# A one-core decode kernel: the first loads split in another way, and the last weight in other chunks

## The chip, the cores and the metric

The kernel runs on one core of a Trainium2 chip. The metric is the device time of one execution in microseconds. A core has an engine for matrix products (PE; its weight loads are told apart as PEld), a vector engine (DVE), a scalar engine (ACT), GpSimd (POOL) and a sync engine (SP), which in this kernel issues nearly all transfers. Sixteen DMA engines per core carry the transfers. Each transfer from the SP queue is cut into rows, one contiguous row per partition, and the rows are dealt out over the sixteen engines. When an engine has written its share of a transfer it raises that transfer's semaphore; the transfer has landed when all sixteen have.

## What is computed

One token, `x` of 576 numbers, is normalised and goes through two branches whose results are added to it.

```
xn = layernorm(x)                                   # 576
q  = xn @ wq                                        # 576 x 4096: 32 heads of 128
k, v = last 4096 rows of the caches, 16 kv heads    # two q heads share a kv head
A  = softmax(q k^T / sqrt(128)) v  -> 4096  @ wo    # 4096 x 576
z  = gelu(xn @ w_in)                                # 576 x 4608, halves z1, z2 of 2304
B  = (z1 * (w_sp * layernorm(z2) + b_sp)) @ w_out   # 2304 x 576
out = x + A + B                                     # 576
```

All inputs are bf16. What has to be read from memory is 51 MB: `wq` 4.7 MB, `w_in` 5.3 MB, the windows of K and V 16.8 MB each, `wo` 4.7 MB and `w_out` 2.7 MB.

## The kernel before

**Tiles.** `wq_t` and `win_t` hold the two first weights with 128 partitions, one contiguous row of 36,864 or 41,472 bytes for each partition. K and V come in four pieces each, called quads (`kn0` to `kn3`, `v0` to `v3`), of four kv heads and 4 MB. A quad has 128 partitions with a row of 32,768 bytes each. The quads share a pool of three buffers, `kvpool`: K0, K1 and V0 take the three, and each later one waits until the buffer that it takes over has been read for the last time. `w_out` is held as two halves of nine rows per partition; the first half is one tile, the second is three tiles, by `WOUT_CHUNKS` (L38). `wo` is two tiles.

**Order of the transfers.** All of these are issued on SP's queue in the order in which the program names them. `load_rows` (L110 to L114) issues a weight in `parts` transfers, the f-th of which holds the partitions f, f + parts, and so on. `load_quad` (L94 to L99) does the same for a quad. The calls of L116 to L120 are the first nine transfers: `wq` in four, `w_in` in one, K0 in two, K1 in one, V0 in one. Three small loads (`xrow`, two elements of `sb_row`, L76 to L78) are issued on ACT's queue at the same time. Later, K2 is issued behind the first quad's work, V1 and K3 behind the second's, V2 and V3 behind the third's, and then the output weights in the order `w_out` first half, `wo` in two, `w_out` second half in three (L440 to L444).

**Semaphores.** The transfers of both queues take eight landing semaphores in turn. A transfer that takes one up again first waits, on the issuing engine, for the landing of the transfer that had it before. What stands behind it on that queue waits with it.

**Order of the work on PE.** PE and SP run in the order in which the program is written (`manual_schedule`, L107). PE makes the statistics of `x`, then `xn_times(wq_t, ...)` (L238), the columns of q (L244), `xn_times(win_t, ...)` (L257), the columns of z (L268), and then quad by quad the transposes of K (`transpose_k`, L328), the scores (L345), the transposes of the probabilities (L362) and the products with V (`pv`, L384). Filler products (`spin`, L455) stand at a few places behind the third quad. The end is `project` (L470), which adds one row of `wo` or `w_out` at a time, as two products, into two PSUM rows: `wo` in two chunks, then the second half of `w_out` chunk by chunk (L499, L500). Two casts (L503, L504) and one transfer of 1,152 bytes (L505) write the result.

Every product of `xn_times` contracts over all 128 partitions, so it needs every part of its weight, however this is split by partitions.

Of the kernel before, what the change touches and what calls it, by code (L numbers as in the profile page):

```python
# [34 lines left out]
NZ1 = 18  # L35
KV_BUFS = 3
WO_CHUNKS = ((0, 20), (20, 32))
WOUT_CHUNKS = ((0, 0, 9), (1, 0, 5), (1, 5, 8), (1, 8, 9))  # L38


@with_exitstack
def kernel(
# [14 lines left out]
    nc = tc.nc  # L57
    P = nc.NUM_PARTITIONS
# [26 lines left out]
    wq_t = wpool.tile([P, 9, 2048], BF16, name="wq")  # L85
    win_t = wpool.tile([P, 9, FH], BF16, name="win")
# [7 lines left out]
    def load_quad(cache, jq, nm, parts):  # L94
        tile_ = kvpool.tile([P, 128, DH], BF16, name=f"{nm}{jq}", tag="kv")
        dst, src = tile_[:].rearrange("p t d -> p (t d)"), quad_rows(cache, jq)
        for f in range(parts):
            nc.sync.dma_start(dst[f:P:parts, :], src[:, f:4:parts, :])
        return tile_  # L99

    def load_k(jq, parts=1):
        kn_tiles[jq] = load_quad(A_k_cache, jq, "kn", parts)

    def load_v(jq, parts=1):
        v_tiles[jq] = load_quad(A_v_cache, jq, "v", parts)
# [1 line left out]
    order = tc.manual_schedule(engines={PE, SP})  # L107
    ctx.enter_context(order)

    def load_rows(tile_, src, parts):  # L110
        for f in range(parts):
            nc.sync.dma_start(
                tile_[f:P:parts].rearrange("p k c -> p (k c)"),
                src.rearrange("m c -> (m c)").rearrange("(p n) -> p n", p=P)[f:P:parts, :])  # L114

    load_rows(wq_t, A_wq, 4)  # L116
    load_rows(win_t, B_w_in, 1)
    load_k(0, 2)
    load_k(1)
    load_v(0)  # L120


    ident = const.tile([P, P], BF16, name="ident")
# [185 lines left out]
    wout_sb = []  # L309
    for i, t0, t1 in WOUT_CHUNKS:  # L310
        n = (t1 - t0) * D
# [122 lines left out]
    def load_wout(n):  # L434
        i, t0, t1 = WOUT_CHUNKS[n]
        nc.sync.dma_start(  # L436
            wout_sb[n],
            B_w_out[ZC * i:ZC * (i + 1), :].rearrange("(p t) n -> p t n", t=9)[:, t0:t1, :])

    load_wout(0)  # L440
    for n, (r0, r1) in enumerate(WO_CHUNKS):
        nc.sync.dma_start(wo_sb[n][:], A_wo.rearrange("(p r) n -> p r n", r=32)[:, r0:r1, :])  # L442
    for n in range(1, len(WOUT_CHUNKS)):
        load_wout(n)  # L444
# [8 lines left out]
    def spin(n):  # L453
        for _ in range(n):
            nc.tensor.matmul(  # L455
                spare[:], lhsT=ident[:], rhs=q_bf[:].rearrange("p g c x -> p (g c x)"), start=True, stop=True)
# [17 lines left out]
    def project_b(n, ts):  # L474
        i, t0, t1 = WOUT_CHUNKS[n]
        for t in ts:
            k = 9 * i + t
            project(hv[:, k:k + 1], wout_sb[n][:, t - t0, :], last=(k == NZ1 - 1))
# [16 lines left out]
    for n, (r0, r1) in enumerate(WO_CHUNKS):  # L495
        for r in range(r0, r1):
            project(oT_all[:, r:r + 1], wo_sb[n][:, r - r0, :])
        spin((4, 0)[n])
    for n in range(1, len(WOUT_CHUNKS)):  # L499
        project_b(n, range(WOUT_CHUNKS[n][1], WOUT_CHUNKS[n][2]))  # L500

# [35 lines left out]
```

The softmax here doesn't subtract the row's maximum and nothing guards it: scores larger than these inputs give would overflow.

## Time and profile before

| what | value |
|---|---|
| time before, median of nine runs (lowest, highest) | 127.57 us (127.44, 127.79) |
| the profiled execution: its own time, its span | 127.79 us, 126.0 us |
| busy share of the span: PE, PEld, DVE, ACT, POOL | 74%, 53%, 35%, 32%, 2% |
| bytes moved, mean rate over the span | 51.11 MB, 406 GB/s |
| SP's queue: share of sixteen engines' span | 94.7% |
| mean granted clock of PE | 0.932 of full speed |

The span runs from the first instruction on the core to the last. Times inside it are counted from its start. The profile has a page with the shares, the span in forty slices, the DMA queues, the chain of work that ended last and the costliest groups of instructions. The trace behind it also gives what each engine and SP's queue waited for, a timeline, tables by stretch of time, and the start, length and size of every row that a DMA engine moved.

### The profile page before, as it was taken

What the parts mean: (1) busy time and instruction counts of PE and PEld (TensorE: products, weight loads), DVE (VectorE), ACT (ScalarE), POOL (GpSimd) and SP (SyncE); (2) the same over time, 40 slices, a digit from 0 to 9 for tenths busy, and PEclk for the clock granted to TensorE, in tenths of its full rate; (3) what the DMA queues carried; (4) which work ended last, traced back from release to release, by engine and by line L of the source; (5) the groups of instructions that cost most, each with busy time, mean ns of one, the idle gap of its engine ahead of it and who ended that gap; (6) DMA issues with size and microseconds to landing.
All of it is one profiled execution on the core that took longest, in us unless ns stands there. A gap on an engine that the chain in (4) does not pass through costs nothing.

```text
span 126.0 us, 2538 instructions
## 1 busy us (share of the span) xinstructions
PE 93.2 (74%) x1110; PEld 66.8 (53%) x1110; DVE 44.6 (35%) x127; ACT 40.9 (32%) x49; POOL 2.8 (2%) x10
## 2 busy tenths in 40 slices
PE   0110398358859999997967999506999999999982
PEld 0010138324859977885637785206878554554551
DVE  6062001102135364497539453452245245010001
ACT  3000001001003578876833679200656910100001
POOL 5010000000000000001000000000000000000000
PEclk9999999999855599999999999995599999999999
DMA  6889999979999899998999999999999999999960
GB/s 188 375 375 492 492 421 421 421 343 484 416 416 489 354 489 403 416 489 359 479 395 432 447 416 453 406 437 447 411 450 416 432 411 408 458 433 390 410 253 0
DMA packets 2386, 51.11 MB, mean 406 GB/s; under 512 B 326, under 2 KB 456, under 8 KB 712
## 3 DMA queue, kind: packets, MB, share of 16 engines
q1 hardware_dynamic: 2370, 50.96, 94.7%
q8 instruction: 8, 0.13, 0.4%
q14 instruction: 2, 0.02, 0.0%
q10 hardware_dynamic: 6, 0.00, 0.0%
HBM read 50.96 MB, written 0.00 MB: 404 GB/s over the span
## 4 chain that ended last, share of the span: by engine, by line
DMA 75%; PE 19%; ACT 2%; SPq 2%; issue 1%; ACTq 0%
DMA kn<-in_A_k_cache_dram 39%; DMA wout<-in_B_w_out_dram 32%; PE ktps L328 14%; DMA wq<-in_A_wq_dram 4%; PE sps L345 2%; ACT kT L332 1%; PE ops L384 1%; SPq L436 1%; PE fin L397 1%; SPq L442 1%; PE sps L470 1%; PE ptps L362 0%; ACT res L504 0%; ACTq L332 0%
## 5 line engine op out<-in xcount | busy, mean ns | idle before, releaser
L328 PE MATMUL ktps<-ident,kn 128*128 128x128 bf16 x512 | 35.9, 235 | 10.0 <-DMA kn<-in_A_k_cache_dram 9.2
L328 PEld LDWEIGHTS <-kn 128*128 128x128 bf16 x512 | 33.1, 106 | 14.8 <-DMA kn<-in_A_k_cache_dram 8.0
L332 ACT COPY kT<-ktps 128x1024 bf16<-128x1024 bf16 x32 | 31.3, 1014 | 24.1 <-PE ktps L328 24.1
L334 DVE COPY kT<-ktps 128x1024 bf16<-128x1024 bf16 x32 | 21.9, 689 | 20.5 <-PE ktps L328 20.5
L232 PEld LDWEIGHTS <-xz 128*32 128x32 bf16 x90 | 4.1, 140 | 13.9 <-issue 12.3
L345 PE MATMUL sps<-kT,q_bf 128*32 128x512 bf16 x128 | 10.7, 383 | 0.8 <-ACT kT L332 0.8
L232 PE MATMUL sps<-wq,xz 128*32 128x512 bf16 x36 | 4.5, 631 | 6.6 <-DMA wq<-in_A_wq_dram 6.6
L455 PE MATMUL spare<-q_bf,ident 128*128 128x512 bf16 x36 | 8.5, 380 | 0.0
L365 DVE TENSOR_TENSOR ptq<-ptps,own 128x128 bf16<-128x128 bf16 x32 | 4.6, 214 | 10.8 <-PE ptps L362 10.8
L384 PE MATMUL ops<-v,ptq 128*32 128x512 bf16 x128 | 8.2, 380 | 0.0
L371 DVE TENSOR_REDUCE psum_all<-ptq 128x8 f32<-128x1024 bf16 x4 | 7.9, 1971 | 0.1
L232 PE MATMUL zps<-win,xz 128*32 128x384 bf16 x54 | 4.3, 490 | 3.7 <-DMA win<-in_B_w_in_dram 3.7
L241 ACT COPY zrow<-sps 128x512 f32<-128x512 f32 x1 | 0.6, 585 | 15.9 <-PE sps L232 15.9
L455 PEld LDWEIGHTS <-ident 128*128 128x128 bf16 x36 | 3.2, 98 | 4.5 <-issue 1.2
L345 PEld LDWEIGHTS <-q_bf 128*32 128x32 bf16 x128 | 3.1, 94 | 4.4 <-issue 2.6
L390 ACT COPY on<-ops 128x512 f32<-128x512 f32 x4 | 2.3, 585 | 9.4 <-PE ops L384 9.4
L397 PE MATMUL fin<-on,sel 128*32 128x128 f32 x32 | 5.1, 312 | 0.3 <-ACT on L390 0.2
L384 PEld LDWEIGHTS <-ptq 128*32 128x32 bf16 x128 | 3.6, 96 | 3.1 <-issue 0.4
L504 ACT CAST res<-sps 1x320 bf16<-1x320 f32 x1 | 0.4, 416 | 14.6 <-PE sps L470 14.6
L268 PE MATMUL fin<-join,zrow 128*128 128x4 f32 x18 | 4.4, 379 | 0.9 <-DVE zrow L261 0.9
L268 PEld LDWEIGHTS fin<-join,zrow 128*128 128x128 f32 x18 | 4.4, 335 | 1.2 <-ACT zrow L260 1.2
L470 PE MATMUL sps<-wo,oT_all 128*1 128x256 bf16 (+1 forms) x64 | 4.7, 285 | 0.4 <-DMA wo<-in_A_wo_dram 0.2
(88 smaller groups left out, 50.1 us busy)
## 6 DMA issues: line engine op xcount, KB each, us to landing
v<-in_A_v_cache_dram SPq DMA_DIRECT2D x4, 4096.0 KB, 15.3
kn<-in_A_k_cache_dram SPq DMA_DIRECT2D x3, 4096.0 KB, 19.5
win<-in_B_w_in_dram SPq DMA_DIRECT2D x1, 5184.0 KB
wq<-in_A_wq_dram SPq DMA_DIRECT2D x4, 1152.0 KB, 8.7
kn<-in_A_k_cache_dram SPq DMA_DIRECT2D x2, 2048.0 KB, 31.6
wo<-in_A_wo_dram SPq DMA_DIRECT2D x1, 2880.0 KB
wo<-in_A_wo_dram SPq DMA_DIRECT2D x1, 1728.0 KB
wout<-in_B_w_out_dram SPq DMA_DIRECT2D x1, 1296.0 KB, 28.6
```

The source lines that it names most:

```text
L232: nc.tensor.matmul(banks[b][32 * i:32 * i + 32, 0:n], lhsT=xz[:, k, :], rhs=w[:, k, c0:c0 + n], start=(t == 0), stop=(k >= 7), tile_positi ...
L268: nc.tensor.matmul(fin[:, MZ + 4 * t:MZ + 4 * t + 4], lhsT=zv[:, t, :], rhs=join[:], start=True, stop=True,)
L328: nc.tensor.transpose(tps[:, s, :], kn[:, 32 * c + 8 * f + s, :], ident[:])
L332: nc.scalar.copy(kT[:], src)
L334: nc.vector.tensor_copy(kT[:], src)
L345: nc.tensor.matmul(sps[b][32 * i:32 * i + 32, :], lhsT=q_bf[:, g, c, :], rhs=parts[f // 2][:, 512 * (f % 2):512 * (f % 2) + 512], start=(c ...
L365: nc.vector.tensor_tensor(ptq[:, c, b, :, :].rearrange("p i (s x) -> p i s x", x=8), ptps[:, 4 * b:4 * b + 4, :].rearrange("p s (i r) -> p ...
L371: nc.vector.tensor_reduce(out=psum_all[:, 8 * g:8 * g + 8], in_=ptq[:].rearrange("p c b i (s x) -> p x (c b i s)", x=8), op=ALU.add, axis=AXX,
L384: nc.tensor.matmul(ops[32 * i:32 * i + 32, :], lhsT=ptq[:, c, b, i, :], rhs=v[:, t0:t0 + 4, :], start=(c == 0 and b == 0), stop=(c == 3 an ...
L397: nc.tensor.matmul(oall, lhsT=sel[:, a, 32 - 8 * g:64 - 8 * g], rhs=on_sb[:, DH * a:DH * (a + 1)], start=(g == 0 and a == 0), stop=(g == 3 ...
L455: nc.tensor.matmul(spare[:], lhsT=ident[:], rhs=q_bf[:].rearrange("p g c x -> p (g c x)"), start=True, stop=True)
L470: nc.tensor.matmul(outp[g], lhsT=lhsT, rhs=rhs[:, c0:c1], start=first, stop=last, tile_position=(0, 32 * g),)
```

## The change

`wq` is loaded in one transfer, not four. `w_in`, K1 and V0 are loaded in two transfers each, the even and the odd partitions, not in one; K0 stays in two. The number of transfers ahead of K2 is nine in both. The second half of `w_out` is cut after the sixth and the eighth row per partition, not after the fifth and the eighth. The tiles of the first loads, the order of the rest and every computation are as before.

```diff
-WOUT_CHUNKS = ((0, 0, 9), (1, 0, 5), (1, 5, 8), (1, 8, 9))
+WOUT_CHUNKS = ((0, 0, 9), (1, 0, 6), (1, 6, 8), (1, 8, 9))
...
-    def load_rows(tile_, src, parts):
-        for f in range(parts):
-            nc.sync.dma_start(
-                tile_[f:P:parts].rearrange("p k c -> p (k c)"),
-                src.rearrange("m c -> (m c)").rearrange("(p n) -> p n", p=P)[f:P:parts, :])
-
-    load_rows(wq_t, A_wq, 4)
-    load_rows(win_t, B_w_in, 1)
+    nc.sync.dma_start(
+        wq_t[:].rearrange("p k c -> p (k c)"), A_wq.rearrange("m c -> (m c)").rearrange("(p n) -> p n", p=P))
+    for f in range(2):
+        nc.sync.dma_start(
+            win_t[f:P:2].rearrange("p k c -> p (k c)"),
+            B_w_in.rearrange("m c -> (m c)").rearrange("(p n) -> p n", p=P)[f:P:2, :])
     load_k(0, 2)
-    load_k(1)
-    load_v(0)
+    load_k(1, 2)
+    load_v(0, 2)
```

## The prediction

> **What bounds the kernel now.** I read the page first: the slices of DMA, the queues, and the chain that ended last.
>
> ```profile
> span 126.0 us, 2538 instructions
> ...
> DMA  6889999979999899998999999999999999999960
> ...
> q1 hardware_dynamic: 2370, 50.96, 94.7%
> ...
> DMA 75%; PE 19%; ACT 2%; SPq 2%; issue 1%; ACTq 0%
> ```
>
> The DMA engines are busy in nearly every slice, and three quarters of the chain is transfers. PE's 74% says nothing against this: a busy engine can still have slack. The table by stretches of time shows how full the engines are; its last two columns are the mean busy share of the sixteen DMA engines and GB/s. Rows are booked where they start, so a short stretch can exceed 1.
>
> ```profile
> 1.70:2.05 0.35, 0.00 (x0) 0.00 (x0) 0.18 (x2) 0.16 (x1) 0.35 (x2) 1.00 0.00 0
> 2.05:2.50 0.45, 0.00 (x0) 0.00 (x0) 0.45 (x2) 0.45 (x1) 0.26 (x1) 1.00 3.44 983
> ...
> 26.30:57.20 30.90, 27.49 (x330) 22.85 (x330) 13.54 (x33) 13.78 (x17) 0.00 (x0) 0.83 0.99 427
> 57.20:104.50 47.30, 38.41 (x541) 28.04 (x541) 22.88 (x54) 24.26 (x29) 0.55 (x1) 0.93 1.00 430
> 104.50:119.00 14.50, 14.14 (x137) 7.49 (x135) 1.74 (x4) 0.59 (x1) 0.00 (x0) 1.00 0.99 422
> ```
>
> Nothing moves before 2.05 us, and from 26.3 to 119 us the engines are full at 422 to 430 GB/s. So a load that was ready earlier would not move faster. Next SP's queue, to see whether the engines ever run out of issued work:
>
> ```profile
> 0.72 2.61 SPq L112 DMA_DIRECT2D wq<-in_A_wq_dram  x4
> 3.38 0.60 SPq L112 DMA_DIRECT2D win<-in_B_w_in_dram  x1
> 4.02 3.47 SPq L98 DMA_DIRECT2D kn<-in_A_k_cache_dram  x3
> 7.54 0.62 SPq L98 DMA_DIRECT2D v<-in_A_v_cache_dram  x1
> 49.47 0.53 SPq L98 DMA_DIRECT2D kn<-in_A_k_cache_dram  x1
> ```
>
> All of the first nine transfers are queued by 8.2 us. K2 is issued at 49.47 us, while V0 lands only at 57.18 (the trace's landing of its semaphore), so K2 is queued 7.7 us ahead of its turn. Last the chain and PE's timeline at the end:
>
> ```profile
> 82.62 40.17 DMA wout<-in_B_w_out_dram
> 122.79 0.04 issue
> 122.83 0.72 PE sps L470 x8
> ```
> ```profile
> 121.76 0.84 PE L470 MATMUL sps<-wout,hv 128*1 128x256 bf16 x10
> 122.83 0.71 PE L470 MATMUL sps<-wout,hv 128*1 128x256 bf16 x8 [0.22 <-DMA wout<-in_B_w_out_dram]
> ```
>
> PE waits for each chunk of `w_out` and is through 0.7 us after the second lands. The kernel's time is therefore the start of the stream, plus 51 MB at the engines' rate, plus a short tail. In the trace's landings the last chunk reaches the sixteen engines' marks from 120.89 to 123.16 us: the slowest engine sets the end. The lag comes from 16 KB fetches of instructions, eight of which occupy some engine for 0.88 to 0.96 us and stretch its next row from 1.21 to about 1.7 us.
>
> **The change part by part.** The sum is made on the profiled execution: 127.79 us, of which 126.0 are span and 1.79 lie around it. It is the highest of the nine runs, 0.22 above the median of 127.57, so the forecast is the median plus the sum.
>
> *Bytes and rows.* None is added. Each engine still moves eight rows of `wq`, eight of `w_in`, eight of each quad. The rate does not depend on the split: `wq`'s quarters land at 6.28, 9.00, 11.74 and 14.48 us, 2.73 us apart for 1.18 MB (432 GB/s); K0's halves take 4.85 us each (landing of the typical engine 31.3, 36.1), and whole K1 takes 9.7 (45.8). Cost 0.
>
> *Issues.* Nine issues ahead of K2 before and after. With 32 rows one takes 0.56 to 0.70 us on SP, with 64 rows 0.55 to 0.58, with 128 rows 0.53 to 0.62; the last chunk of `w_out` (128 rows) took 0.327 and the output (one row) 0.308. So the number of rows hardly enters. Only the first issue stands before an idle queue. From its start to the first row are 1.36 us (0.72 to 2.08).
>
> *The start with a whole `wq`.* The trace has no 128-row transfer onto idle engines, so I bound it. Lower end: the sixteen first rows took 1.47 to 2.24 us, the rows after them 1.37 to 1.38. If that excess came from the three further issues that follow at once (1.33 to 3.33 us), a single transfer could win back up to 0.7 us. Upper end: from the end of the issue to the first row passed 0.80 us for 32 rows (1.28 to 2.08), and 0.41 for the one row of `xrow` (1.21 to 1.62, on ACT's queue). If the 0.39 between them were time per row, 128 rows would add three times that, +1.17. The nearest rows are the issues of 128 rows, which cost what those of 32 cost; I take 0 and keep -0.7 and +1.17.
>
> *`sb_row`.* Its two scalars share an engine with `wq`: their 2-byte rows stand at 3.97 and 5.36 us between rows of `wq`, and a product at L155 waits for them until 6.06. Behind a single transfer they may come as now, or, at worst, after all eight rows (14.1 us), 8.7 us later. What hangs on them is ready at 10.2 (the last write of `xz`) and would be at 18.9, so the products with `wq` (14.6) would start 4.3 us late. PE idles 3.7 us before `w_in` and 1.6 before K0's transposes, 5.3 in all. Cost 0 at both ends, and the cover ends 1.0 us later still.
>
> *A new wait on SP.* The semaphores are taken in turn. Before, K0's second half took up that of the first quarter of `wq` and waited 1.7 us for it, until 6.28. After, K1's second half takes up that of the whole `wq`, about 14.5 us. V0's two halves are queued behind it on SP, and nothing else until K2. The engines reach K1's second half when `wq`, `w_in`, K0 and K1's first half are moved, about 41 us (K0's end 36.1 plus 4.85). Cost 0, with 26 us of cover. PE waits for both halves of `w_in`, K0, K1 and V0; their last landings stay, and K1 (47.5) and V0 (57.2) land ahead of their first use at 50.9 and 62.4 us.
>
> *The tail.* An engine's rows of the second half took 220, 135 and 51 ns (5,760, 3,456 and 1,152 bytes). Per byte that is 37 ns a KB, so the six-row chunk takes 262 and the two-row one 93: the same sum. The first chunk lands 8 x 42 ns later, at 122.06 and not 121.72; the others at 122.79 and 123.16 as now. PE streams a row's two products in about 0.135 us: twelve products from 122.10 end their issue at 122.91, four more at 123.18. The last two start when the last chunk is there, 123.20, as now (123.198). Cost 0 to +0.02.
>
> Sum: 0.0 (start) + 0.0 (issues, `sb_row`, SP's wait) + 0.02 (tail): 127.6 us on the median's scale.
>
> **A rule against the change.** The Trainium skill, "DMA: Bandwidth & Descriptors", section "Rules for kernel authors", says not to split a transfer into two by partitions, since both halves use the same sixteen engines; use one for all 128. The same page ("Anatomy of one DMA") gives a transfer prepared by GpSimd a fixed cost of about 2 us, mostly the wait for the last write; SP's transfers are prepared otherwise. By it three more halves would cost up to 6 us and the joined `wq` would give back 6: an estimate of 0 again. The quarters that landed 2.73 us apart show that this cost overlaps in a full queue.
>
> **The rivals.**
> *Late start (slower).* Rows are prepared one by one, and a whole `wq` starts later. For it: 0.80 against 0.41 us above. Against: 0.327 against 0.308 us of issue. Nothing behind the start can hide it, since the engines stay full to the end; it decides from 0.25 us, that is from 2.6 ns for each of the 96 further rows. Price 0.25 to 1.17, middle 0.6: 128.2 us.
> *Quieter start (faster).* The slow first rows are due to the crowd of small transfers. Against: the rows that ran while K0, K1 and V0 were issued (6.3 to 8.2 us) took 1.37 to 1.38, so issuing hardly disturbs. Price -0.25 to -0.7: 127.1 us.
> *Another slowest engine (either sign).* The fetches fall on other engines in relation to the late starters (first rows begin 2.08 to 3.10 us). Most engines with one fetch end at 122.45 to 122.86, the last two at 123.11 and 123.16. Even spread: -0.3 to -0.6; a second fetch on a slow engine: +0.5 to +1.4.
> *The tail turns to PE.* If PE cannot take six rows between 122.06 and 123.16, its lag is the price: 0.1 us, inside no change.
>
> **How the numbers follow.** A change below 0.2% (0.26 us) is not told from none. No change 0.32, at 127.6. Late start 0.30, another engine slower 0.11: slower 0.41. Quieter start 0.16, another engine faster 0.11: faster 0.27. No change is the likeliest single case, and its own range is 127.3 to 127.85. The range for 8 in 10 leaves out only the ends: below 126.9 (0.08) and above 128.5 (0.10).
>
> **What would show it.** Right: the first row of `wq` at 2.1 us, `wq` landed at 14.4 to 14.6, SP's wait for `wq` about 10 us, the first chunk of the second half landing some 0.3 us later and the last at 123.0 to 123.4. Late start: no bytes until 2.3 us or later, and every landing shifted by the same amount. Quieter start: first rows near 1.4 us. Another engine: the spread of the last landing not 2.3 us. What would make it wrong altogether: a stretch after 26 us with engines below 0.99 busy, which would mean that the split does change the rate.

## The result and the profile after

The changed kernel takes 127.19 us (median of 18 runs, 126.99 to 127.32), against 127.51 us for the kernel before beside it (54 runs). The ratio is 0.9972, with a 95% interval of 0.9964 to 0.9979: faster by 0.28%, some 0.35 us. The likeliest case of the prediction was no change; the time lies inside its range, and on the side that it gave 27 chances in 100. Of one kernel below, the one with `wq` in blocks, two executions of six took 1.9 us longer than the other four, and its profile is of one of the two.

The page of the changed kernel, the lines that answer to those of before:

```profile
span 125.6 us, 2539 instructions
...
DMA  6899999989989899999999989899898999999960
...
q1 hardware_dynamic: 2370, 50.96, 95.0%
...
DMA 72%; PE 21%; SPq 3%; ACT 1%; issue 1%; DVE 0%; ACTq 0%
```

The DMA engines still bound the kernel. Their table by stretches has the same columns as before; the last two are the mean busy share of the sixteen engines and GB/s.

```profile
1.70:2.05 0.35, 0.00 (x0) 0.00 (x0) 0.15 (x2) 0.25 (x1) 0.35 (x2) 1.00 3.72 948
2.05:2.50 0.45, 0.00 (x0) 0.00 (x0) 0.45 (x2) 0.45 (x1) 0.26 (x1) 1.00 1.31 410
26.30:57.20 30.90, 27.27 (x331) 22.49 (x332) 14.07 (x35) 14.31 (x17) 0.00 (x0) 0.78 0.99 426
57.20:104.50 47.30, 39.87 (x542) 29.33 (x542) 22.63 (x52) 23.83 (x29) 0.56 (x1) 0.89 1.00 429
```

The first line is the news. Between 1.70 and 2.05 us nothing moved before; now nine of the sixteen first rows begin there, the first at 1.76 us and not 2.08. The full stretches run at the rate of before. SP's queue on the timeline shows what precedes it:

```profile
0.72 0.40 SPq L110 DMA_DIRECT2D wq<-in_A_wq_dram  x1
1.19 1.17 SPq L113 DMA_DIRECT2D win<-in_B_w_in_dram  x2
2.40 12.56 SPq L98 DMA_DIRECT2D kn<-in_A_k_cache_dram  x4
15.00 1.25 SPq L98 DMA_DIRECT2D v<-in_A_v_cache_dram  x2
48.94 0.54 SPq L98 DMA_DIRECT2D kn<-in_A_k_cache_dram  x1
```

The whole `wq` is issued in 0.40 us; its first quarter took 0.56. The 12.56 us for K0 and K1 hold the wait for `wq`'s landing (10.1 us on SP). At the end, the chain and PE's timeline:

```profile
83.40 38.26 DMA wout<-in_B_w_out_dram
121.66 0.04 issue
121.70 1.40 PE sps L468 x16
123.10 0.04 issue
123.14 0.41 DVE res L501
```
```profile
121.70 1.39 PE L468 MATMUL sps<-wout,hv 128*1 128x256 bf16 x18 [0.26 <-DMA wout<-in_B_w_out_dram]
```

PE now takes all eighteen products in one run. The first cast begins at 123.12 us, not 123.56; its line before, and then after:

```profile
123.56 0.41 DVE L503 CAST res<-sps 1x256 bf16<-1x256 f32 x1 [12.22 <-PE sps L470]
```
```profile
123.12 0.42 ACT L502 CAST res<-sps 1x320 bf16<-1x320 f32 x1 [14.31 <-PE sps L468]
```

The trace's rows and landings give the difference stage by stage:

```
                                      before    after
sixteen first rows begin, mean          2.40     2.09
wq's last rows end, mean               13.91    13.70
V3's last rows end, mean              104.60   104.29
last chunk lands, first engine        120.89   120.75
last chunk lands, last engine         123.16   122.73
span                                  126.0    125.6
```

An advance of 0.2 to 0.3 us is there from the first rows and is carried through to V3. At the last chunk it is 0.14 us on the first engine and 0.43 on the last; these are one execution each.

### The profile page after: what moved, and what is told of

It reads as the page before. It is cut to its first block, busy times and chain, and to the rows that moved or that the text cites. A ratio compares the mean times of both kernels' runs of the same rounds, so it can differ in the third digit from the quotient of the medians.

```text
span 125.6 us, 2539 instructions
## 1 busy us (share of the span) xinstructions
PE 92.6 (74%) x1110; PEld 66.0 (53%) x1110; DVE 44.7 (36%) x127; ACT 41.0 (33%) x49; POOL 2.8 (2%) x10
## 4 chain that ended last, share of the span: by engine, by line
DMA 72%; PE 21%; SPq 3%; ACT 1%; issue 1%; DVE 0%; ACTq 0%
DMA kn<-in_A_k_cache_dram 41%; DMA wout<-in_B_w_out_dram 30%; PE ktps L326 14%; PE sps L343 2%; ACT kT L330 1%; PE ops L382 1%; PE fin L395 1%; PE sps L468 1%; SPq L113 1%; SPq L440 1%; SPq L98 0%; SPq L434 0%; PE ptps L360 0%; DVE res L501 0%; SPq L110 0%
## 5 line engine op out<-in xcount | busy, mean ns | idle before, releaser
L326 PE MATMUL ktps<-ident,kn 128*128 128x128 bf16 x512 | 36.9, 239 | 8.8 <-DMA kn<-in_A_k_cache_dram 8.1
L326 PEld LDWEIGHTS <-kn 128*128 128x128 bf16 x512 | 34.0, 108 | 13.4 <-DMA kn<-in_A_k_cache_dram 7.0
L153 PE MATMUL fin<-sb_row,one_row 1*128 1x2 bf16 x1 | 0.2, 178 | 6.6 <-DMA sb_row<-in_B_b_sp_dram 6.6
```

The lines of the kernel that those rows point to most:

```text
L326: nc.tensor.transpose(tps[:, s, :], kn[:, 32 * c + 8 * f + s, :], ident[:])
```

## The experiments

The ratios are to the kernel before, run on the same chip; each has its 95% interval. A ratio of 0.001 is 0.13 us.

**One part at a time.** The first three runs take the parts of the change: the chunks of `w_out` alone, the first loads alone, and of these the whole `wq` alone. The fourth has the halves without the whole `wq`.

```diff
-WOUT_CHUNKS = ((0, 0, 9), (1, 0, 5), (1, 5, 8), (1, 8, 9))
+WOUT_CHUNKS = ((0, 0, 9), (1, 0, 6), (1, 6, 8), (1, 8, 9))
```

> The kernel before with the second half of w_out in parts of six, two and one rows; the first loads as before. Start theory (the whole wq puts its first row in motion at 1.76 us and not 2.08, and all that follows is earlier): ratio 1.000 (0.9995 to 1.0005), first row at 2.08 us, last landing of w_out 123.0 to 123.3 us. Tail theory (the gain is in the last chunks): ratio 0.997. Halves theory (the gain is in splitting w_in, K1 and V0): ratio 1.000.

Measured: 127.39 us, 0.9993 (0.9984 to 1.0002). The first row at 2.07 us. Not told from no change, and not the gain.

The second run undoes only that line in the changed kernel.

> The changed kernel with the second half of w_out cut as before, in five, three and one rows. Start theory: ratio 0.997 to 0.998, first row at 1.76 us, last landing 122.7 us. Tail theory: 1.000. Halves theory: 0.997.

Measured: 127.19 us, 0.9980 (0.9971 to 0.9989); first row at 1.75 us, last landing 122.61 us. The first loads carry the gain.

```diff
-    load_rows(wq_t, A_wq, 4)
+    load_rows(wq_t, A_wq, 1)
```

> The kernel before with wq alone in one transfer; w_in, K1 and V0 whole, K0 in halves, w_out as before. Start theory: ratio 0.997 to 0.998, the first issue 0.40 us long, the first row at 1.76 us. Tail theory and halves theory: 1.000.

Measured: 127.41 us, 0.9992 (0.9983 to 1.0001). The issue took 0.395 us and the first row began at 1.74 us, as the start theory has it, but the time hardly moved.

```diff
-    load_rows(win_t, B_w_in, 1)
+    load_rows(win_t, B_w_in, 2)
     load_k(0, 2)
-    load_k(1)
-    load_v(0)
+    load_k(1, 2)
+    load_v(0, 2)
```

> The kernel before with w_in, K1 and V0 in halves; wq still in quarters, w_out as before. Start theory: ratio 1.000, first row at 2.08 us. Halves theory: 0.997. Tail theory: 1.000.

Measured: 127.63 us, 1.0015 (1.0006 to 1.0024); first row at 2.09 us. Slower, which no theory expected.

So the start theory had the mechanism, yet the whole `wq` alone gave back most of it. Where it went stands at the very end. On the timeline of the run with `wq` alone whole:

```profile
122.93 0.42 ACT L504 CAST res<-sps 1x320 bf16<-1x320 f32 x1 [14.55 <-PE sps L470]
123.40 0.31 SPq L505 DMA_DIRECT2D out_dram<-res  x1
```

From the output's issue to the end of the span are 2.14 us there (123.40 to 125.54), and 2.19 in the run with the halves; before it was 1.97 (124.03 to 126.00), and 1.98 after. The trace's semaphore waits on SP show why. At the end SP checks the landing semaphores in a fixed order, two at a time, 0.06 us a check:

```
wq alone whole (output raises 106)        before (output raises 109)
123.397  output issued                    124.035  output issued
123.761  104, 103                         124.400  104, 103
124.536  106, 102   <- waited             124.464  106, 102
124.598  108, 100                         124.525  107, 100
124.662  109, 101                         124.590  108, 101
124.724  110, 107                         125.186  109, 110   <- waited
```

The eight semaphores are taken in turn, so the number of transfers decides which of them the output gets. With nine first transfers it is the one checked last, and the other checks pass while the output is on its way. With six, three checks follow its landing (0.19 us); with twelve it is the first pair, and four follow (0.25 us). From the output's issue to the end, 0.17 and 0.22 us of this show.

**The count held at nine.**

```diff
-    load_rows(wq_t, A_wq, 4)
+    load_rows(wq_t, A_wq, 1)
...
-    load_v(0)
+    load_v(0, 4)
```

> wq in one transfer, w_in and K1 whole, K0 in halves, V0 in four: nine first transfers again, so that the output transfer has the same turn of the eight semaphores as before. w_out as before. Start theory with its end correction (the whole wq starts the rows 0.33 us earlier; in the run with wq alone whole, 0.19 us of this was given back at the end, since the output's semaphore was checked second of five and three more checks of 0.06 us followed): ratio 0.9975 to 0.9985, first row 1.75 us, nothing checked after the output's landing but the last semaphore. Rival, that the gain needs w_in and K1 in halves: ratio 0.999 to 1.000.

Measured: 127.19 us, 0.9977 (0.9968 to 0.9986); first row at 1.75 us; 1.98 us from the output's issue to the end. Between this run and the one with `wq` alone whole lie 0.0015, 0.19 us; 0.16 us of it stand in the traces between the output's issue and the end (2.14 and 1.98 us). The halves of `w_in` and K1 are not needed for the gain. The reverse check adds two transfers to the changed kernel:

```diff
-    load_v(0, 2)
+    load_v(0, 4)
```

> The changed kernel with V0 in four transfers, eleven first transfers and not nine. Start theory with the end correction: first row 1.75 us as before, but the output's semaphore comes up second in the checks at the end and three more follow, 0.06 us each: 0.19 us more than the changed kernel, ratio 0.9985 to 0.9990. If the number of transfers does not matter: 0.997.

Measured: 127.36 us, 0.9982 (0.9971 to 0.9993). The first row began at 1.74 us; the output raised the semaphore of the second check, and from its issue to the end were 2.13 us. The loss in the trace is 0.15 us (2.13 against 1.98), where 0.19 was expected. The ratio lies a little below the expected 0.9985 to 0.9990; its interval holds these, and it leaves out the 0.997 of no effect only by a hair.

**Why a whole `wq` starts sooner.** The quarters differ from the whole in the number of rows and in the step from one partition to the next. Two runs separate them, each with nine first transfers.

```diff
-    load_rows(wq_t, A_wq, 4)
+    for f in range(4):
+        nc.sync.dma_start(
+            wq_t[32 * f:32 * f + 32].rearrange("p k c -> p (k c)"),
+            A_wq.rearrange("m c -> (m c)").rearrange("(p n) -> p n", p=P)[32 * f:32 * f + 32, :])
```

> The kernel before, but the four quarters of wq are blocks of 32 neighbouring partitions, not every fourth partition. If the step between the partitions makes the first issue long: issue about 0.40 us, first row about 1.75 us, ratio 0.998. If it is the number of rows in the first transfer, or how many transfers wq has: issue 0.56 us, first row 2.08 us, ratio 1.000.

```diff
-    load_rows(wq_t, A_wq, 4)
-    load_rows(win_t, B_w_in, 1)
+    load_rows(wq_t, A_wq, 2)
+    load_rows(win_t, B_w_in, 2)
     load_k(0, 2)
-    load_k(1)
+    load_k(1, 2)
```

> wq in two transfers of every other partition, w_in, K0 and K1 in halves, V0 whole: nine first transfers. If the step makes the first issue long: issue 0.53 to 0.57 us, first row 2.05 to 2.1 us, ratio 0.9995 to 1.0005. If a larger first transfer starts earlier: first row 1.85 to 2.0 us, ratio 0.999.

SP's timeline of the run with blocks, and the table's stretch 1.70 to 2.05 us:

```profile
0.72 1.93 SPq L117 DMA_DIRECT2D wq<-in_A_wq_dram  x4
```
```profile
1.70:2.05 0.35, 0.00 (x0) 0.00 (x0) 0.13 (x1) 0.26 (x1) 0.35 (x2) 1.00 5.21 1159
```

The same two of the run with two halves:

```profile
0.72 1.19 SPq L112 DMA_DIRECT2D wq<-in_A_wq_dram  x2
```
```profile
1.70:2.05 0.35, 0.00 (x0) 0.00 (x0) 0.20 (x2) 0.16 (x1) 0.35 (x2) 1.00 0.00 0
```

The group's time is that of all its issues: 1.93 us for four, 1.19 for two. With blocks of 32 neighbouring partitions the first issue took 0.39 us and the first row began at 1.73 us. With 64 rows of every other partition it took 0.56 us and the first row began at 2.06 us; the time was 127.52 us, 1.0005 (0.9996 to 1.0014). So neither the number of rows nor that of the transfers makes the start late; the step between the partitions does. The rows that are read have the same step in memory, and no run has the one step without the other.

The blocks however took 138.62 us, the median of all six; the ratio, by the four of 138.41 to 138.64 us, is 1.0867 (1.0853 to 1.0881). The start theory's 0.998 missed this altogether. Two stretches of `wq`'s load, of the profiled execution:

```profile
8.00:14.00 6.00, 0.15 (x1) 0.10 (x1) 0.00 (x0) 0.00 (x0) 0.00 (x0) 1.00 0.96 203
14.00:20.00 6.00, 0.62 (x3) 0.50 (x2) 2.77 (x22) 0.00 (x0) 0.55 (x1) 1.00 0.97 197
```

The engines are as busy as ever and move half: a row of 36,864 bytes took 2.67 to 2.90 us and not 1.36. Eight rows an engine, 1.3 to 1.5 us more each, come to 10.4 to 12.3 us; the four lost 11.1. In this trace `wq`'s last rows end at 24.52 us on average, 10.6 later than before. Its rows of `w_in` and the first of K0 were longer too (1.72 and 1.35 us, for 1.53 and 1.21), which fits the longer time of this one execution. This is what the step of the quarters was good for: as long as `wq` is cut by partitions, the step keeps the rate. The Trainium skill, "SBUF — State Buffer", section "Door 1: The DMA port swizzle", says that the partitions 0 to 31 reach eight of sixteen ports; the 197 to 203 GB/s here, somewhat under half of 432, agree. That the ports are the cause is not shown here, since the blocks are neighbours in memory too. The page also says ("Can I just issue two DMAs to hit both halves?"): "The only way to hit all 16 ports is one transfer spanning all 128 partitions." Here 32 rows at every fourth partition ran at the full 432 GB/s, so a transfer has to reach over the partitions but need not hold all of them.

**Whether ACT's small loads delay the first issue.** SP and ACT issue at the same instant, 0.72 us. This kernel issues ACT's three loads 1.5 us later, from 2.24 us on.

```diff
     sb_row = const.tile([1, 2], BF16, name="sb_row")
+    warm = const.tile([1, 4], BF16, name="warm")
+    nc.vector.memset(warm[:], 0.0)
+    nc.scalar.copy(xrow[:, 0:4], warm[:])
+    nc.scalar.copy(sb_row[:], warm[:, 0:2])
     nc.scalar.dma_start(xrow[:], x_flat)
```

> The changed kernel with the three small loads on ACT's queue issued behind two short copies on ACT, about 2.3 us instead of 0.72 us, so that SP issues wq with no other issue beside it. If the two issues get in each other's way: first issue 0.30 to 0.35 us, first row 1.65 us, ratio 0.996. If they do not: first row 1.75 us, ratio 0.997. If sb_row now comes too late: the products with wq begin about 2 us later, still hidden, ratio 0.997.

Measured: 127.73 us, 1.0024 (1.0014 to 1.0034). The first issue took 0.407 us and the first row began at 1.75 us: the issues are not in each other's way. But the kernel was slower than the changed one, by 0.5 us in the medians and 0.7 in the ratios, which nobody expected. In its trace most rows of K, V and `wo` from V0 on (45 us) are a little longer: 1.216 us or more for one of K or V, against 1.213, 0.859 against 0.855 and 0.520 against 0.516 for `wo`'s. Those of `wq`, `w_in`, K0 and K1 are as long as before (1.364, 1.533, 1.213 and 1.213 us, the median of each). The new tile takes 32 bytes and had moved all tiles that SP loads, from multiples of 256 bytes within a partition to 32 bytes behind. The next kernel sets 224 bytes more aside.

```diff
     xrow = const.tile([1, D], BF16, name="xrow")
+    pad2 = const.tile([P, 112], BF16, name="pad2")
```

> The kernel of the run with the small loads later, with 224 more bytes set aside per partition, so that every loaded tile starts at a multiple of 256 bytes again (in that run all of them were 32 bytes off, by the 32 bytes of the tile that was added). If the 32 bytes made the rows slower (1.216 and not 1.213 us a row of K and V): rows 1.213 us and a ratio of 0.997 again. If the later small loads cost the time: rows 1.216 us, ratio 1.002.

Measured: 127.21 us, 0.9969 (0.9957 to 0.9981), with rows of 1.213, 0.855 and 0.516 us. The table by stretches while the output weights are loaded, first the shifted tiles, then the aligned ones:

```profile
104.50:119.00 14.50, 14.11 (x135) 7.57 (x135) 2.34 (x4) 0.59 (x1) 0.00 (x0) 1.00 0.99 419
```
```profile
104.50:119.00 14.50, 13.74 (x134) 7.38 (x132) 0.75 (x4) 0.58 (x1) 0.00 (x0) 1.00 1.00 427
```

So the 32 bytes cost the time, and the later small loads cost nothing, although the products with `wq` waited for them in this run (2.3 us for `xz`). Between the two traces the rows from K0 on add up to 0.38 us an engine. The first engine's last landing is 0.38 us later (120.99 and 120.61), the last engine's 0.74 (123.35 and 122.61). The fetches of instructions were longer as well, 0.99 to 1.10 us for 0.88 to 0.96; what makes up the rest on the last engine is not shown.

**The tail.** One run has the whole `wq`, V0 in four, and the new chunks; the other makes the first chunk longer still.

> wq whole, w_in and K1 whole, K0 in halves, V0 in four, and the second half of w_out in six, two and one rows. Start theory plus a small gain of the tail (0.0 to 0.1 us): ratio 0.9970 to 0.9978. Start theory alone: 0.9977. Halves theory: 0.999 to 1.000.

Measured: 127.23 us, 0.9970 (0.9957 to 0.9984). This is not told from the changed kernel, and no version tried here is clearly better.

```diff
-WOUT_CHUNKS = ((0, 0, 9), (1, 0, 6), (1, 6, 8), (1, 8, 9))
+WOUT_CHUNKS = ((0, 0, 9), (1, 0, 7), (1, 7, 8), (1, 8, 9))
```

> The changed kernel with the second half of w_out in seven, one and one rows. By the sum of the prediction: the seven-row chunk lands 0.34 us later than the six-row one, at about 122.0 us, and PE needs 0.95 us for its fourteen products and 0.27 for the last four, so that it ends 0.1 to 0.2 us behind the last landing instead of with it: ratio 0.998 to 0.999. If PE has room to spare there: 0.997.

Measured: 127.48 us, 0.9992 (0.9984 to 1.0001), a loss of 0.25 us against the changed kernel, a little more than the expected 0.998 to 0.999. PE at the end:

```profile
122.06 1.39 PE L468 MATMUL sps<-wout,hv 128*1 128x256 bf16 x18 [0.62 <-DMA wout<-in_B_w_out_dram]
```

The seven rows land at 122.01 us, as the expectation had it; PE streams the eighteen products in 1.39 us and ends 0.68 us behind the last landing (122.76). In the changed kernel it ended 0.39 behind, before 0.40 (casts against last landing). Six rows are the most that PE takes without falling behind.

The chunks of six, two and one compare three times with those of five, three and one: 0.9993 to 1, 0.9972 to 0.9980, 0.9970 to 0.9977. Each time it is 0.0007 or 0.0008, some 0.09 us, and no single comparison tells it from nothing. The profiles show only 0.02 us of it, from the last landing to the casts. Whether the rest is real stays open.

## Why the prediction was right or wrong

*What bounds the kernel*: right. The engines stay full from 26 to 119 us, and what is won at the start arrives at the end.

*Bytes and rows*: right. Halves, quarters at a step and wholes run at one rate. It was right only because of the step, which the prediction did not see.

*The start with a whole `wq`*: this is the step that failed. The prediction took 0, between -0.7 and +1.17; measured is -0.32 (first row 1.76 for 2.08 us), 0.16 of it in the issue and 0.16 between the issue's end and the row. The bounds held it, the choice did not. The choice went by the number of rows: issues of 128 rows cost what those of 32 cost. The rows that were compared hid the difference. The quarters had a step and were first on the queue; the 128-row issues stood behind them and took 0.597 us for `w_in`. With nothing stepped ahead of it the same issue of `w_in` takes 0.41 (runs with a whole `wq` and a whole `w_in`). A step is not all that lengthens an issue further back: the fourth block of `wq`, with no step ahead of it, took 0.58 us, and whole K2 0.53. The 0.80 us from issue to row, against 0.41 for `xrow`, was read as a price per row and so as a risk of a later start; that sign was wrong (with the whole `wq` it is 0.63). One sign that the prediction gave for no change did not tell: `wq` landed at 14.41 us, inside the 14.4 to 14.6 named, with its last rows 0.21 us earlier on average.

*The rivals.* The quieter start had the sign and, with -0.25 to -0.7, the size, but not the mechanism. It would have shown as first rows near 1.4 us long; they took 1.37 to 2.75, no shorter than before. They begin earlier instead. The late start is excluded by every run with a whole `wq`. Another slowest engine is not the cause, as the traces show when they are taken together. Four kernels load `wq` with a step (before, the chunks alone, the halves alone, `wq` in two), and eight load it whole, with every tile at a multiple of 256 bytes. The means, in us:

```
                                        step    whole   earlier by
sixteen first rows begin                2.30     2.00     0.30
V3's last rows end                    104.49   104.22     0.26
last chunk lands, first engine        120.93   120.63     0.30
last chunk lands, last engine         122.95   122.61     0.34
between the two last                    2.02     1.98
```

The advance is that of the first rows at every stage, and the spread over the engines is the same. The 0.43 and 0.14 us of the two profiles above are scatter around it.

*Issues*: half right. Their number does cost nothing on SP at the start. It decides at the end which semaphore the output gets, worth 0 to 0.22 us in the traces. The prediction held it as no cost for nine against nine, which was true without its being known why.

*`sb_row`*: the bounds held and the cost is 0. The product of L155 (L153 after) came at 9.91 us, 3.85 later, and the last of `xz` at 13.87. The products with `wq` still waited for `wq`, from 14.45 us.

*SP's new wait*: right. K2 was issued at 48.94 us, as early as before. Of SP's waits, the one for the whole `wq` took 10.1 us:

```profile
SPq L98 <- DMA wq<-in_A_wq_dram: 10.1, 1, 10.1
```

*The tail*: right to 0.02 us by its sum; the run with seven rows confirms the price of a row and the edge that it named.

## What to carry to other kernels

When transfers bound a kernel from its first byte, the form of the very first one counts: give it whole, neighbouring partitions, and compare it in the profile by when the first row begins. Where a tile must be cut by partitions, let each part reach over all of them, and begin what is loaded at multiples of 256 bytes (32 bytes behind is the only other place tried here). Before a gain or a loss of 0.1 or 0.2% is put down to a change, compare the time from the output's issue to the end, since the number of transfers alone can move it.

## What the runs showed of the hardware that was not expected

- The first transfer of the queue takes longer to issue with a step between its partitions: 0.56 to 0.57 us against 0.39 to 0.41, and its first row begins 2.06 to 2.09 us into the span against 1.73 to 1.76, with 32 or 64 rows against 32 or 128.
- Sixteen engines that write 32 neighbouring partitions take 2.67 to 2.90 us for a row of 36,864 bytes, in the one profile of it; at every fourth partition it is 1.36 to 1.38.
- Tiles 32 bytes off a multiple of 256 made most rows of K, V and `wo` from 45 us on some 3 to 4 ns longer or more, of 13,824 bytes and of 32,768 alike, and the kernel 0.5 to 0.7 us slower; rows before that were not longer. Why is not shown. The Trainium skill, "DMA: Bandwidth & Descriptors", section "How a descriptor splits into AXI transactions", says of reads that a transaction has to start at a multiple of 256 bytes, so that a piece that begins elsewhere also costs bytes that it does not use. Taken over to writes this would be paid by every row of a shifted tile; `wq`'s, `w_in`'s, K0's and K1's did not pay it.
- At the end SP checks the landing semaphores in a fixed order at 0.06 us a check, and what follows the output's own check comes on top of the time: 0.15 to 0.17 us for three checks and 0.22 for four.
